# Infinite-attention then low-rank mixer on one core: scores of a pair in one row-tiled stretch, PSUM as one ring of eight banks, down tiles whole

## The chip, the core and the metric

One of the cores of a Trainium2 chip runs the whole program. The metric is the device time of one execution in microseconds (us), as the median of several runs. A profile is one more execution, with the trace taken by the hardware profiler; it has a time of its own, and the span in it is from the first to the last instruction.

The engines are named as in the profile: PE is TensorE (PEld its weight loads), DVE is VectorE, ACT is ScalarE, POOL is GpSimd, SP is SyncE, which issues most of the DMAs. Each engine works through its instructions in program order; what it waits for comes from the others over semaphores.

## The reference

Attention over 4 batches and 8 heads, with 768 positions and 64 channels a head, where a position sees only the first 8 positions and the 96 last ones, with a linear bias; its output, with the heads side by side (768 x 512 a batch), goes through a mixer: a low-rank product along the sequence (rank 32) is added, then an MLP of 512 to 2048 to 512 with ReLU is added.

```python
scores = scale * np.matmul(q, k.transpose(0, 1, 3, 2))
keep = is_global | is_local          # first 8 keys, or the 96 last ones
scores = np.where(keep, scores + bias, -1000000000.0)
a = softmax(scores)                  # over the keys
x = heads_side_by_side(a @ v)        # (4, 768, 512)
...
h = x.transpose(0, 2, 1) @ U @ V
u = x + h.transpose(0, 2, 1)
out = u + np.maximum(u @ w_ch1, 0.0) @ w_ch2
```

## The kernel before

**Pairs.** Two heads of one batch, which fill 128 partitions as 2 x 64, are a pair: 16 pairs, numbered i, four (NP) a batch. The sequence is six blocks of 128. A block of queries needs the scores of its own block and, for the blocks 1 to 5, those of a block kA that holds the block before it, with the global keys copied over its first rows. That is 11 tiles of 128 x 128 for each head, kept side by side as 1408 columns, computed in three chunks (512, 512, 384 columns).

**One pair's steps.** `st_T` (for the pairs up to 7) turns q and k with matmuls and copies them out of PSUM; `turn` and `st_K` do that for the later ones with DMA transposes. `scores` (L320) writes a chunk of both heads to two PSUM banks. The matmuls of the heads contract over 64 rows, one over the upper, one over the lower half of the array, and are issued in turn. Pairs 0 to 3 add the bias on PE and take the exponential straight from PSUM (`st_SE`); for the pairs 4 to 15, `s_dve` (L366) adds it on DVE while it writes the chunk to SBUF, and `st_E` (L378) takes the exponential of a whole head on ACT. `st_V` (L383) multiplies by v, with a column of ones for the sum: 11 matmuls of 65 columns a head, then a reciprocal (L399), a multiply (L407) on DVE and a cast to f16 on POOL (L408).

**The mixer's steps.** `st_M1` (L411) multiplies a pair's 128 channels by U, six matmuls, and DVE copies the result out. `st_M3` (L450) multiplies that by V, six matmuls into two banks, adds it on DVE to x (L462), and POOL casts the sum (L465). U and V hold rank 32 in 128 rows, the rest zeros. `st_X` (L443) turns the cast sum with a DMA transpose into uT. The MLP of half a batch (g) is 16 up tiles and 3 down tiles. An up tile (L480) is four matmuls of 384 columns, with a ReLU on ACT (L484). A down tile (L500) is 16 matmuls of 512 columns, cut into four parts, or for the last tile into two halves of the columns; DVE adds x (L506) and SP sends the block out. Batch 0 has one matmul more in every down tile, for its V product.

**The order.** It is written out by hand, and `manual_schedule` keeps it. The prologue (L569 to L610) does the attention of batch 0; it also computes chunk 0 of pair 4. The loop over i from L614 does the steps of pair i, `st_V` and `st_M1` and `st_M3` and `st_X` of pair i - 1, and between them calls `fill(n)`, which issues n pieces from two queues: up tiles, and parts of down tiles. `queue_ff` fills the queues; a batch's pieces are queued when all of its pairs have been turned into uT, for batch b in the iteration of pair 4b + 5. `held` keeps the down tiles back until the iteration of pair 7. Up tiles may run ahead of the down tiles of the half before (`room`), and `ahead` deals about four ups to three parts. What is left after the loop is issued in its order.

**PSUM.** Eight banks in four groups: `sc` 2, `ob` 1 (the output of `st_V`), `cps` 2 (down tiles), `th` 3 (everything else: transposes, up tiles, U and V products). A tile waits until the bank of its group that was taken longest ago has been read.

Of the kernel before, what the change touches and what calls it, by code (L numbers as in the profile page):

```python
# [20 lines left out]
def kernel(  # L21
# [13 lines left out]
    nc = tc.nc  # L35
# [38 lines left out]
    def ps_sc(tag="sc"):  # L74
        return psum.tile([P, 512], FP32, name="sc", tag=tag, bufs=2)

    def ps_ob():
        return psum.tile([P, 512], FP32, name="ob", tag="ob", bufs=1)

    def ps_cps(name):  # L80
        return psum.tile([P, 512], FP32, name=name, tag="cps", bufs=2)

    def ps_th(name, dtype=FP32, cols=512):
        return psum.tile([P, cols], dtype, name=name, tag="th", bufs=3)

# [64 lines left out]
    def warm(n):  # L150
        wps = ps_cps("warm")
        for _ in range(n):
            nc.tensor.matmul(wps, zw[:, 0:P], zw, start=True, stop=True)
# [77 lines left out]
    def st_T(i):  # L231
# [4 lines left out]
        for st in (stq, stk):  # L236

            tp = ps_th("tp", FP16, S)
# [81 lines left out]
    def scores(i, c, on_pe):  # L320
        kT, kA, qT = kts[i], kas[i], qts[i]
        scs = [ps_sc("cps" if on_pe and (i + c) % 2 else "sc") for _ in range(2)]
        c0 = 512 * c
        tot = min(512, W - c0)
        r0 = 256 if c else 0
        if on_pe:
            for hi in range(2):
                nc.tensor.matmul(
                    scs[hi][:, 0:tot], slI[:, 2 * (i % NP) + hi],
                    rel16.rearrange("p a c -> p (a c)")[:, r0:r0 + tot], start=True, stop=False,  # L330
                )
        for kb in (2 * c, 2 * c + 1):
            o = 256 * kb - c0
            for hi in range(2):
                r = slice(hi * D, (hi + 1) * D)
                nc.tensor.matmul(  # L336
                    scs[hi][:, o:o + P], kT[r, kb * P:(kb + 1) * P], qT[r, kb * P:(kb + 1) * P],
                    start=(o == 0 and not on_pe), stop=(o + P == tot),
                )
            if kb == NSB - 1:  # L340
                continue
            for hi in range(2):
                r = slice(hi * D, (hi + 1) * D)
                nc.tensor.matmul(  # L344
                    scs[hi][:, o + P:o + 2 * P], kA[r, kb], qT[r, (kb + 1) * P:(kb + 2) * P],
                    start=False, stop=(o + 2 * P == tot),
                )
        return [(sc, c0, tot, r0) for sc in scs]

    def st_SE(i, c):  # L350
# [4 lines left out]
        for hi, (sc, c0, tot, _) in enumerate(scores(i, c, True)):  # L355
# [6 lines left out]
    def s_dve(i, hi, got):  # L362
        sc, c0, tot, r0 = got
        if c0 == 0:
            sps[i, hi] = scp.tile([P, W], FP32, name=f"sp{hi}", tag=f"sp{hi}", bufs=1)
        nc.vector.scalar_tensor_tensor(  # L366
            out=sps[i, hi][:, c0:c0 + tot], in0=sc[:, 0:tot],
            scalar=qk_scale / slope[2 * (i % NP) + hi], in1=relf[:, r0:r0 + tot],
            op0=ALU.mult, op1=ALU.add,
        )  # L370

    def st_S(i, c):
        for hi, got in enumerate(scores(i, c, False)):
            s_dve(i, hi, got)
# [8 lines left out]
    def st_V(i, hi):  # L383
        b, h = i // NP, 2 * (i % NP) + hi
        ep, vt, vA = eps.pop((i, hi)), vts[i], vas[i]
        obf = ps_cps("ob") if (i, hi) == (NP - 1, 1) else ps_ob()
# [24 lines left out]
    def st_M1(i):  # L411
        b, dc = i // NP, i % NP
        ch = slice(dc * P, (dc + 1) * P)
        tps = ps_th("tmp_ps")
        for n in range(NSB):
            nc.tensor.matmul(  # L416
                tps[:, 0:P], u16[:, n], x16s[b][:, dc, n],
# [4 lines left out]
    def st_M2(i):  # L422
        b, dc = i // NP, i % NP
        ch = slice(dc * P, (dc + 1) * P)
        for g in range(2):
            ups = ps_th("ups")
# [23 lines left out]
    def st_M3(i):  # L450
        b, dc = i // NP, i % NP
        ch = slice(dc * P, (dc + 1) * P)
        for g in range(2):
            ups = ps_th("ups")
            for t in range(NTG):
                n = NTG * g + t
                nc.tensor.matmul(  # L457
                    ups[:, t * P:(t + 1) * P], v16w[:, n * P:(n + 1) * P], tmps[b][:, ch],
                    start=(t == 0), stop=(t == NTG - 1),
                )  # L460
            dst = xs[b][:, NTG * g:NTG * (g + 1), ch]
            nc.vector.tensor_tensor(  # L462
                dst, ups[:, 0:GT].rearrange("p (t d) -> p t d", t=NTG), dst, ALU.add
            )
        nc.gpsimd.tensor_copy(x16s[b][:, dc], xs[b][:, :, ch])  # L465
# [3 lines left out]
    def queue_ff(b, g):  # L469
# [4 lines left out]
        def mk_up(jt):  # L474
            def go():
                if jt == 0:
                    cell["htr"] = ffp.tile([P, NJC, GT], FP16, name="htr", tag="htr")
                hps = ps_th("hps")
# [8 lines left out]
        def mk_down(t, part):  # L487
            n = NTG * g + t

            def go():  # L490
                if part == 0:
                    cell["cps"] = ps_cps("cps")
                    if b == 0:
                        nc.tensor.matmul(
                            cell["cps"], v16w[:, n * P:(n + 1) * P], tmp16,
                            start=True, stop=False,
                        )
                cps, htr = cell["cps"], cell["htr"]
                for jc in range(4 * part, 4 * part + 4):
# [4 lines left out]
                if part == NJC // 4 - 1:  # L504
                    osb = ffp.tile([P, DM], FP32, name="osb", tag="osb", bufs=3)
                    nc.vector.tensor_tensor(osb, cps, x_sb[:, n], ALU.add)  # L506
                    nc.sync.dma_start(out[b, n * P:(n + 1) * P, :], osb)
            return go

        def mk_last(t, half):  # L510
            n = NTG * g + t
            cs = slice(half * (DM // 2), (half + 1) * (DM // 2))

            def go():
                cps = ps_cps("cps")[:, 0:DM // 2]
                htr = cell["htr"]
                for jc in range(NJC):
                    nc.tensor.matmul(  # L518
                        cps, htr[:, jc, t * P:(t + 1) * P], w2_16[:, jc, cs],
                        start=(jc == 0), stop=(jc == NJC - 1),  # L520
                    )
                osb = ffp.tile([P, DM], FP32, name="osb", tag="osb", bufs=3)
                nc.vector.tensor_tensor(osb[:, cs], cps, x_sb[:, n, cs], ALU.add)
                nc.sync.dma_start(out[b, n * P:(n + 1) * P, cs], osb[:, cs])
# [4 lines left out]
        for t in range(NTG):  # L529
            if (b, g, t) == (B - 1, 1, NTG - 1):  # L530
                for half in range(2):
                    downs_q.append((mk_last(t, half), (b, g)))
                continue
            for part in range(NJC // 4):
                downs_q.append((mk_down(t, part), (b, g)))

    ahead, held = [0], [True]

    def fill(n):
        for _ in range(n):  # L540
            down = downs_q and not held[0] and not any(w == downs_q[0][1] for _, w in ups_q)
            room = ups_q and (not downs_q or downs_q[0][1] == ups_q[0][1]
                              or ups_q[0][1] in follows(downs_q[0][1]))
            if down and room:
                if ahead[0] > 0:
                    ahead[0] -= 4
                    downs_q.popleft()[0]()
                else:
                    ahead[0] += 3
                    ups_q.popleft()[0]()  # L550
            elif down:
                downs_q.popleft()[0]()
            elif room:
                ups_q.popleft()[0]()
            else:
# [48 lines left out]
    first = scores(NP, 0, False)  # L604
# [4 lines left out]
    for hi in range(2):  # L609
        s_dve(NP, hi, first[hi])  # L610
# [3 lines left out]
    for i in range(NP, NPAIR + 2):  # L614
        b, hp = divmod(i, NP)
        live = i < NPAIR
        n = 1 if i < 2 * NP + 1 else 2
# [11 lines left out]
        if i == NP + 1:  # L629
            load_qk(NP + 4)  # L630
        fill(2)
# [17 lines left out]
        if i > NP + 1 and (i - 2) % NP == NP - 1:  # L649
            queue_ff((i - 2) // NP, 0)  # L650
            queue_ff((i - 2) // NP, 1)
            ahead[0] = 1
        if i == NPAIR + 1:
            break
        fill(n)
        if live:
            st_S(i, 2)
            if i < NPE:
                st_P(i)
        if i + 1 < NPAIR:  # L660
            if i + 1 >= NPE:
                st_K(i + 1)
# [5 lines left out]
        fill(1)  # L668
        if i > NP:
            st_M1(i - 1)  # L670
        if live:
            st_E(i, 0)
        fill(2)
        if i > NP:
            st_M3(i - 1)
            st_X(i - 1)
        if live:
            st_E(i, 1)
        if i + 2 < NPAIR and i + 2 >= NPE:
            turn(i + 2)  # L680
        fill(1 + n)
# [38 lines left out]
```

## Time and profile before

| | us |
|---|---|
| runs, median of 3 | 245.56 (245.24 to 245.64) |
| the profiled execution | 243.5 |
| its span | 241.6 |
| PE busy | 228.9 |
| DVE busy | 126.7 |
| ACT busy | 114.2 |
| POOL busy | 79.0 |

The page divides the span into 40 slices of 6.04 us, and gives the busy share of each engine in tenths. PE is at 8 or 9 in nearly all of them; DVE, ACT and POOL are busiest in the first half, while there are pairs to do, and nearly idle at the end, where only the MLP is left. A busy PE counts the time from a matmul's start to its modelled end, so that matmuls that follow one another overlap; the distance from one start to the next tells more. In a group's line, the columns are line, engine, operation, output and inputs, shape and count, then busy us and mean ns of one, then the idle time of the engine before them and what ended most of it. In a timeline's line they are start, length, the group, and, in brackets, idle time before it and what ended that.

### The profile page before, as it was taken

The numbers are of one execution on the slowest core, as the hardware profiler recorded it, in microseconds if no ns is written. First come the engines' busy times: TensorE is split into PE (matmuls) and PEld (weight loads), VectorE is DVE, ScalarE is ACT, GpSimd is POOL, SyncE is SP. The second block draws the span as 40 slices with busy tenths as digits, with TensorE's granted clock in tenths as the row PEclk, the third lists the DMA queues.
The fourth block names the chain that finished last, engine by engine and source line by source line (L and its number), as shares of the span: only waits on it lengthen the run. The fifth ranks groups of instructions, "written<-read, shape, count | busy, mean of one in ns | idle before, by whom it ended". The sixth has DMA issues, their size and how long they took to land.

```text
span 241.6 us, 4863 instructions
## 1 busy us (share of the span) xinstructions
PE 228.9 (95%) x1952; PEld 127.9 (53%) x1952; DVE 126.7 (52%) x269; ACT 114.2 (47%) x196; POOL 79.0 (33%) x122
## 2 busy tenths in 40 slices
PE   7789899889999999999999999999999999999994
PEld 3355654555554545555555555555565555555553
DVE  6878975848486867565747574745432111011121
ACT  6686548676650403765453407482733234543300
POOL 6379837657272524151515142212111000000000
PEclk9999999999999999999999999999999999999999
DMA  6999999999596979985949582721121200111022
GB/s 186 314 309 324 226 241 272 197 230 217 116 207 148 236 216 161 240 198 136 241 111 212 150 230 69 184 56 37 57 67 33 87 34 12 43 43 42 7 85 87
DMA packets 86030, 36.61 MB, mean 152 GB/s; under 512 B 74136, under 2 KB 82552, under 8 KB 86008
## 3 DMA queue, kind: packets, MB, share of 16 engines
q1 hardware_dynamic: 81480, 32.01, 53.2%
q0 software_dynamic: 4528, 4.29, 10.9%
q8 instruction: 15, 0.25, 0.4%
q14 instruction: 7, 0.06, 0.1%
HBM read 27.46 MB, written 6.29 MB: 140 GB/s over the span
## 4 chain that ended last, share of the span: by engine, by line
PE 76%; DMA 9%; POOL 5%; ACT 5%; DVE 2%; issue 2%; SPq 0%; POOLq 0%
PE cps L500 33%; PE hps L480 31%; DMA w<-in_moe_w_ch_dram 5%; PE sc L336 3%; DMA vst<-in_v_dram 3%; ACT ep L378 2%; ACT htr L484 2%; PE ob L394 2%; DMA kst<-in_k_dram 2%; PE cps L518 1%; PE ob L390 1%; PE tmp_ps L416 1%; POOL v L126 1%; POOL vA L277 1%; PE sc L344 1%
## 5 line engine op out<-in xcount | busy, mean ns | idle before, releaser
L484 ACT ACTIVATE htr<-hps 128x384 f16<-128x384 f32 x128 | 61.8, 491 | 88.6 <-PE hps L480 87.4
L480 PE MATMUL hps<-uT,w 128*128 128x384 f16 x512 | 98.2, 326 | 1.2 <-ACT htr L484 0.8
L500 PE MATMUL cps<-w,htr 128*128 128x512 f16 x368 | 90.8, 379 | 0.0
L480 PEld LDWEIGHTS <-w 128*128 128x128 f16 x512 | 46.7, 98 | 34.9 <-issue 2.1
L366 DVE SCALAR_TENSOR_TENSOR sp<-sc,relcat 128x512 f32<-128x512 f32 (+1 forms) x72 | 43.2, 642 | 28.7 <-PE sc L344 23.8
L500 PEld LDWEIGHTS <-htr 128*128 128x128 f16 x368 | 34.2, 98 | 33.6
L506 DVE TENSOR_TENSOR osb<-cps,x_sb 128x512 f32<-128x512 f32 x23 | 15.9, 691 | 50.7 <-PE cps L500 50.5
L378 ACT ACTIVATE ep<-sp 128x1408 f16<-128x1408 f32 x24 | 32.7, 1372 | 12.6 <-DVE sp L366 12.6
L408 POOL CAST x<-x_sb 128x384 f16<-128x384 f32 x30 | 15.4, 513 | 60.0 <-DVE x_sb L407 59.8
L465 POOL CAST x<-x_sb 128x768 f16<-128x768 f32 x12 | 9.9, 829 | 34.1 <-DVE x_sb L462 34.1
L462 DVE TENSOR_TENSOR x_sb<-ups,x_sb 128x384 f32<-128x384 f32 x24 | 12.5, 554 | 11.0 <-PE ups L457 10.6
L336 PEld LDWEIGHTS <-kT 64*128 64x128 f16 x192 | 8.2, 93 | 17.6 <-issue 15.6
L407 DVE TENSOR_TENSOR x_sb<-ob,rcp 128x384 f32<-128x384 f32 x30 | 16.7, 558 | 1.0
L336 PE MATMUL sc<-qT,kT 64*128 64x128 f16 x192 | 16.5, 221 | 0.0
L394 PE MATMUL ob<-v,ep 128*128 128x65 f16 x192 | 16.0, 193 | 0.0
L394 PEld LDWEIGHTS <-ep 128*128 128x128 f16 x192 | 13.8, 98 | 2.7 <-issue 0.2
L126 POOL CAST v<-vst 128x768 f16<-128x768 f32 x16 | 13.4, 839 | 5.5 <-DMA vst<-in_v_dram 5.5
L356 ACT ACTIVATE ep<-sc 128x512 f16<-128x512 f32 (+1 forms) x24 | 12.0, 560 | 4.8 <-PE sc L344 3.5
L344 PE MATMUL sc<-qT,kA 64*128 64x128 f16 x160 | 14.2, 216 | 0.0
L390 PE MATMUL ob<-vA,ep 128*128 128x65 f16 x160 | 14.1, 194 | 0.1
L112 POOL CAST k<-kst 128x768 f16<-128x768 f32 x14 | 12.1, 867 | 0.1
L390 PEld LDWEIGHTS <-ep 128*128 128x128 f16 x160 | 11.0, 97 | 2.1
(73 smaller groups left out, 166.3 us busy)
## 6 DMA issues: line engine op xcount, KB each, us to landing
qst<-in_q_dram SPq DMA_DIRECT2D x16, 384.0 KB, 4.0
kst<-in_k_dram SPq DMA_DIRECT2D x16, 384.0 KB, 5.7
vst<-in_v_dram SPq DMA_DIRECT2D x16, 384.0 KB, 5.9
out_dram<-osb SPq DMA_DIRECT2D x23, 256.0 KB, 2.3
w<-in_moe_w_ch_dram POOLq DMA_DIRECT2D x6, 512.0 KB, 8.7
vA<-v SPq DMA_DIRECT2D x8, 152.3 KB, 3.9
w<-in_moe_w_ch_dram POOLq DMA_DIRECT2D x1, 1024.0 KB, 11.6
out_dram<-osb SPq DMA_DIRECT2D x2, 128.0 KB, 1.7
```

The lines of the kernel that those rows point to most:

```text
L126: nc.gpsimd.tensor_copy(vt.rearrange("p n h d -> p h n d")[:, :, :, 0:D], vsts.pop(i).rearrange("p (h n) d -> p h n d", h=2),)
L336: nc.tensor.matmul(scs[hi][:, o:o + P], kT[r, kb * P:(kb + 1) * P], qT[r, kb * P:(kb + 1) * P], start=(o == 0 and not on_pe), stop=(o + P ...
L344: nc.tensor.matmul(scs[hi][:, o + P:o + 2 * P], kA[r, kb], qT[r, (kb + 1) * P:(kb + 2) * P], start=False, stop=(o + 2 * P == tot),)
L366: nc.vector.scalar_tensor_tensor(out=sps[i, hi][:, c0:c0 + tot], in0=sc[:, 0:tot], scalar=qk_scale / slope[2 * (i % NP) + hi], in1=relf[:, ...
L378: nc.scalar.activation(ep, sps.pop((i, hi)), AF.Exp, scale=slope[2 * (i % NP) + hi])
L390: nc.tensor.matmul(ob[:, qi], ep[:, OF[qi - 1]:OF[qi - 1] + P], vA[:, qi - 1, hi], start=True, stop=False,)
L394: nc.tensor.matmul(ob[:, qi], ep[:, DG[qi]:DG[qi] + P], vt[:, qi, hi], start=(qi == 0), stop=True,)
L407: nc.vector.tensor_tensor(xo, ob[:, :, 0:D], rb, ALU.mult)
L480: nc.tensor.matmul(hps[:, 0:GT], w1_16[:, dc, jt * P:(jt + 1) * P], uT[:, dc, ts], start=(dc == 0), stop=(dc == NDC - 1),)
L484: nc.scalar.activation(cell["htr"][:, jt], hps[:, 0:GT], AF.Relu)
L500: nc.tensor.matmul(cps, htr[:, jc, t * P:(t + 1) * P], w2_16[:, jc], start=(b > 0 and jc == 0), stop=(jc == NJC - 1),)
L506: nc.vector.tensor_tensor(osb, cps, x_sb[:, n], ALU.add)
```

## The change

PSUM becomes one ring of eight banks: every tile, whatever it is for, takes the bank that was taken longest ago, through `bank`. A new function `visit(i, m)` does the V product of pair m = i - 2 and then all 22 score matmuls of pair i, without another matmul between them; the V product reads copies of U and V (`ud`, `vd`) in which rank 32 stands twice, from row 0 and from row 64, so that its two banks are written by matmuls over 64 rows each, issued in turn. It takes up to eight banks: two for the V product and six for the scores. DVE reads them in the order: the two of the V product, the three of head 0, the three of head 1. The cast and the DMA transpose of the V product's sum (`st_C`, `st_X`) are issued in iteration m + 2, behind `st_V` of pair i - 1. Down tiles are issued whole. `fill` becomes `ff(units)`: an up tile counts one unit, a down tile five; a down tile is taken when five ups have been issued since (`since`), when there is no up to take, or when the call asks for one first. An iteration calls `ff` with n, n, n, 1 and n units, where n is 2 up to pair 9 and 3 from there. A batch's pieces are queued at the end of the iteration of pair 4b + 5. Chunk 0 of pair 4 leaves the prologue. The diff, cut to its core:

```diff
+    def bank(name, dtype=FP32, cols=512):
+        return psum.tile([P, cols], dtype, name=name, tag="ps", bufs=8)
...
+    ud = cst.tile([P, NSB, P], FP16, name="ud")
+    vd = cst.tile([P, S], FP16, name="vd")
...
+    def operands(i, hi, t):
+        r = slice(hi * D, (hi + 1) * D)
+        kb, off = t // 2, t % 2
+        key = kas[i][r, kb] if off else kts[i][r, kb * P:(kb + 1) * P]
+        return key, qts[i][r, (kb + off) * P:(kb + off + 1) * P]
...
+    def visit(i, m):
+        NB = 2 * NSB - 1
+        if m is not None:
+            bm, dm = m // NP, m % NP
+            ch = slice(dm * P, (dm + 1) * P)
+            ups = [bank("ups") for _ in range(2)]
+            for t in range(NTG):
+                for g in range(2):
+                    r, n = slice(g * D, (g + 1) * D), NTG * g + t
+                    nc.tensor.matmul(
+                        ups[g][:, t * P:(t + 1) * P], vd[r, n * P:(n + 1) * P], tmps[bm][r, ch],
+                        start=(t == 0), stop=(t == NTG - 1),
+                    )
+            for g in range(2):
+                dst = xs[bm][:, NTG * g:NTG * (g + 1), ch]
+                nc.vector.tensor_tensor(
+                    dst, ups[g][:, 0:GT].rearrange("p (t d) -> p t d", t=NTG), dst, ALU.add
+                )
+        if i is None:
+            return
+        got = []
+        for c in range(3):
+            got.append([bank("sc") for _ in range(2)])
+            for t in range(4 * c, min(4 * c + 4, NB)):
+                for hi in range(2):
+                    o = (t % 4) * P
+                    nc.tensor.matmul(
+                        got[c][hi][:, o:o + P], *operands(i, hi, t),
+                        start=(o == 0), stop=(t % 4 == 3 or t == NB - 1),
+                    )
+        for hi in range(2):
+            sp = scp.tile([P, W], FP32, name=f"sp{hi}", tag=f"sp{hi}", bufs=1)
+            sps[i, hi] = sp
+            for c in range(3):
...
+                nc.vector.scalar_tensor_tensor(
...
+    def st_C(i):
+        b, dc = i // NP, i % NP
+        nc.gpsimd.tensor_copy(x16s[b][:, dc], xs[b][:, :, dc * P:(dc + 1) * P])
...
         for t in range(NTG):
...
+            last = (b, g, t) == (B - 1, 1, NTG - 1)
+            downs_q.append(((mk_last if last else mk_down)(t), (b, g)))
+
+    since, held = [0], [True]
+
+    def can_down():
+        return downs_q and not held[0] and not any(w == downs_q[0][1] for _, w in ups_q)
+
+    def can_up():
+        return ups_q and (not downs_q or downs_q[0][1] == ups_q[0][1]
+                          or ups_q[0][1] in follows(downs_q[0][1]))
+
+    def ff(units, down_first=False):
+        while units > 0:
+            if can_down() and (down_first or since[0] >= 5 or not can_up()):
                 downs_q.popleft()[0]()
+                since[0], down_first = max(0, since[0] - 5), False
+                units -= 5
+            elif can_up():
+                ups_q.popleft()[0]()
+                since[0] += 1
+                units -= 1
             else:
                 return
...
     for i in range(NP, NPAIR + 2):
         b, hp = divmod(i, NP)
         live = i < NPAIR
-        n = 1 if i < 2 * NP + 1 else 2
+        m = i - 2 if i - 2 >= NP else None
+        n = 2 if i < 2 * NP + 2 else 3
         held[0] = i < NP + 3
...
-        if live and i > NP:
-            st_S(i, 0)
-        early = {NP: (NP + 2,), NP + 1: (NP + 3,), NP + 2: (NP + 5,)}
+        if i == NP:
+            ff(2)
+        if i <= NPAIR:
+            visit(i if live else None, m)
+        else:
+            visit(None, m)
+        early = {NP: (NP + 2,), NP + 1: (NP + 3, NP + 4), NP + 2: (NP + 5,)}
         for j in early.get(i, (i + 3,)):
             if j < NPAIR:
                 load_qk(j)
         if i + 1 < NPAIR:
             load_v(i + 1)
-        if i == NP + 1:
-            load_qk(NP + 4)
-        fill(2)
+        ff(n, True)
         if NP < i <= NPAIR:
             st_V(i - 1, 0)
         if i + 1 < NPE:
             st_T(i + 1)
         if live:
             cast_v(i)
             st_A(i)
...
-        fill(n)
+        ff(n)
         if live:
-            st_S(i, 1)
-        fill(1)
+            st_E(i, 0)
         if NP < i <= NPAIR:
             st_V(i - 1, 1)
+        if live and i < NPE:
+            st_P(i)
+        if m is not None:
+            st_C(m)
+            st_X(m)
...
+        ff(n)
         if live:
+            st_E(i, 1)
+        if i + 1 < NPAIR and i + 1 >= NPE:
+            st_K(i + 1)
         if i + 2 < NPAIR:
             cast_qk(i + 2, nc.gpsimd)
         if i == NP:
             load_w2(0)
             load_w2(1)
+            nc.gpsimd.memset(vd.bitcast(I32), 0)
+            nc.gpsimd.memset(ud.rearrange("p n c -> p (n c)").bitcast(I32), 0)
+            for r in (0, D):
+                nc.gpsimd.dma_start(vd[r:r + R], moe_V)
+                nc.gpsimd.tensor_copy(ud[:, :, r:r + R], u16[:, :, 0:R])
-        fill(1)
+        ff(1)
-        if i > NP:
+        if NP < i <= NPAIR:
             st_M1(i - 1)
-        if live:
-            st_E(i, 0)
-        fill(2)
-        if i > NP:
-            st_M3(i - 1)
-            st_X(i - 1)
-        if live:
-            st_E(i, 1)
         if i + 2 < NPAIR and i + 2 >= NPE:
             turn(i + 2)
-        fill(1 + n)
+        if m is not None and m % NP == NP - 1:
+            queue_ff(m // NP, 0)
+            queue_ff(m // NP, 1)
+        ff(n)
```

More of the change, by code (lines that the diff above doesn't have):

```diff
@@ L150, in warm @@
     def warm(n):
-        wps = ps_cps("warm")
+        wps = bank("warm")
         for _ in range(n):
@@ L318, with scores @@
     sps, eps, later = {}, {}, []
-    def scores(i, c, on_pe):
+    def scores(i, c):
         kT, kA, qT = kts[i], kas[i], qts[i]
-        scs = [ps_sc("cps" if on_pe and (i + c) % 2 else "sc") for _ in range(2)]
+        scs = [bank("sc") for _ in range(2)]
         c0 = 512 * c
@@ L425, in st_M2 @@
         for g in range(2):
-            ups = ps_th("ups")
+            ups = bank("ups")
             nc.tensor.matmul(
@@ L477, in go @@
                     cell["htr"] = ffp.tile([P, NJC, GT], FP16, name="htr", tag="htr")
-                hps = ps_th("hps")
+                hps = bank("hps")
                 for dc in range(NDC):
@@ L485, in mk_up, with mk_down @@
             return go
-        def mk_down(t, part):
+        def mk_down(t):
             n = NTG * g + t
             def go():
[L491 to L499, printed above, removed]
+                cps, htr = bank("cps"), cell["htr"]
+                if b == 0:
+                    nc.tensor.matmul(
+                        cps, v16w[:, n * P:(n + 1) * P], tmp16, start=True, stop=False,
+                    )
+                for jc in range(NJC):
                     nc.tensor.matmul(
@@ L503, in go, with mk_last @@
                     )
[L504 to L507, printed above, removed]
+                osb = ffp.tile([P, DM], FP32, name="osb", tag="osb", bufs=3)
+                nc.vector.tensor_tensor(osb, cps, x_sb[:, n], ALU.add)
+                nc.sync.dma_start(out[b, n * P:(n + 1) * P, :], osb)
             return go
[L510 removed]
+        def mk_last(t):
             n = NTG * g + t
[L512 removed]
             def go():
[L515 removed]
                 htr = cell["htr"]
[L517 to L521, printed above, removed]
[L522 to L524 removed]
+                osb = ffp.tile([P, DM], FP32, name="osb", tag="osb", bufs=3)
+                for half in range(2):
+                    cs = slice(half * (DM // 2), (half + 1) * (DM // 2))
+                    cps = bank("cps")[:, 0:DM // 2]
+                    for jc in range(NJC):
+                        nc.tensor.matmul(
+                            cps, htr[:, jc, t * P:(t + 1) * P], w2_16[:, jc, cs],
+                            start=(jc == 0), stop=(jc == NJC - 1),
+                        )
+                    nc.vector.tensor_tensor(osb[:, cs], cps, x_sb[:, n, cs], ALU.add)
+                    nc.sync.dma_start(out[b, n * P:(n + 1) * P, cs], osb[:, cs])
             return go
```

121 lines of the change are left out of this document (23 added, 98 removed).

## The prediction

> **What bounds the kernel now.** I read the page first (busy shares, the 40 slices, the chain), then TensorE's timeline, then the other engines in one iteration. The page's lines are engine shares, chain shares, and two groups with count, busy us, mean ns:
>
> ```profile
> span 241.6 us, 4863 instructions
> PE 228.9 (95%) x1952; PEld 127.9 (53%) x1952; DVE 126.7 (52%) x269; ACT 114.2 (47%) x196; POOL 79.0 (33%) x122
> ...
> PE 76%; DMA 9%; POOL 5%; ACT 5%; DVE 2%; issue 2%; SPq 0%; POOLq 0%
> ...
> L480 PE MATMUL hps<-uT,w 128*128 128x384 f16 x512 | 98.2, 326 | 1.2 <-ACT htr L484 0.8
> L500 PE MATMUL cps<-w,htr 128*128 128x512 f16 x368 | 90.8, 379 | 0.0
> ```
>
> TensorE is the bound; the mean ns of one matmul overlap their neighbours, so I price by start-to-start. The timeline around pair 12's first score chunk (start, length, group):
>
> ```profile
> 123.12 1.03 PE L500 MATMUL cps<-w,htr 128*128 128x512 f16 x4
> 124.08 0.23 PE L336 MATMUL sc<-qT,kT 64*128 64x128 f16 x2
> 124.14 0.22 PE L344 MATMUL sc<-qT,kA 64*128 64x128 f16 x2
> 124.20 0.22 PE L336 MATMUL sc<-qT,kT 64*128 64x128 f16 x2
> 124.26 0.22 PE L344 MATMUL sc<-qT,kA 64*128 64x128 f16 x2
> 124.41 0.82 PE L480 MATMUL hps<-uT,w 128*128 128x384 f16 x4
> ```
>
> Two 64-row matmuls run beside each other, a pair of them every 0.056 us. Four down matmuls take 4 x 0.216, so the first would be through at 123.98; the next full-height matmul starts at 124.41. The chunk costs 0.43: 4 x 0.056 = 0.22 of work and 0.20 for going in and out of row tiling. Likewise a chunk of six is 0.37, an up tile (four matmuls) 0.65, a down tile 16 x 0.216 = 3.46, a V step (11 matmuls of 65 columns) 0.34, U product and V product (six matmuls each) 0.34, an st_T 0.68.
>
> From 32.08 (first up) to 238.1 (last matmul issued) are 206.0 us. Adding these prices over all work of that stretch gives 200.0, so about 6.0 are idle, more than half before 62 us; the rest are three waits of 0.8 of the second V product for a bank that an htr holds.
>
> **The saving.** Before, a pair pays 0.43 + 0.43 + 0.37 + 0.34 = 1.57 for scores and V product. After: one stretch of 0.20 + (11 + 3) x 0.056 = 0.98. That is 0.59 for ten pairs (6 to 15), 0.41 for pair 5 (no V product yet), nothing for pair 4 (a chunk lay in the prologue, where the U product waits for DVE anyway), and -0.03 for each of the last two V products, which switch by themselves. Sum 6.2. The new work is 193.9: 128 ups 83.2, 24 downs 84.2, 24 V steps 8.2, 12 U products 4.1, three st_T 2.0, stretches 12.2.
>
> **The fill, where it fails.** In program order, the new `ff` gives (u = up, D = whole down tile): pairs 4 to 6, 11, 9, 9 u. Pair 7: D, D, D, u, uu. `since` stands at 29 by then, so every call takes a D, which counts 5 against a budget of 1 to 3 and overshoots. Pair 8: D, D, D, then nothing: batch 0 is used up. Pair 9: nothing until batch 1 is queued at its end, then uu. Before, the parts were dealt one by one and the last of batch 0 came in pair 9 itself. Pair 13 likewise: D, D, nothing, then uuu. Pair 17 has D, D, which cover its chain.
>
> So in pair 9 the new end of the chain lies open, since the V product of pair 7 moved there from pair 8, and with it the cast and transpose that the ups need. The rows for it, in the old pair 9 (DVE, POOL, SyncE; then microseconds to landing):
>
> ```profile
> 91.18 1.29 DVE L366 SCALAR_TENSOR_TENSOR sp<-sc,relcat 128x512 f32<-128x512 f32 x2 [1.22 <-PE sc L344]
> 92.49 0.20 DVE L399 RECIPROCAL rcp<-ob 128x6 f32<-128x6 f32 x1
> 92.72 0.56 DVE L407 TENSOR_TENSOR x_sb<-ob,rcp 128x384 f32<-128x384 f32 x1
> ```
> ```profile
> 90.48 0.84 POOL L126 CAST v<-vst 128x768 f16<-128x768 f32 x1
> 93.34 0.51 POOL L408 CAST x<-x_sb 128x384 f16<-128x384 f32 x1 [2.02 <-DVE x_sb L407]
> 98.28 0.83 POOL L465 CAST x<-x_sb 128x768 f16<-128x768 f32 x1 [2.88 <-DVE x_sb L462]
> ```
> ```profile
> uT<-x SPq DMA_TRANSPOSE x12, 2.8
> ```
>
> DVE is in order, and the stretch hands it eight evictions before both halves of pair 8: two adds at 0.47, four score tiles at 0.60, two at 0.46 = 4.3; then reciprocal and multiply, 0.78 a half: 5.1 and 5.9. POOL: first half 5.6, cast of v 6.4, second half 6.9 (the U product of pair 8 waits for it), cast of pair 7 at 7.7. SyncE first issues the two vA transfers (0.94 + 0.79) behind the cast of v, so the transpose starts at 8.2 and lands at 11.0. Only then can an up start.
>
> **Walk.** Pairs 4 to 6: idle of 5.4 by the same kind of sum: banks wait for the second head's evictions (0.5 and 1.1, at st_T), a stretch waits for ACT behind an exponential (0.8), the U products wait for POOL (1.35 and 1.6). Pair 7 starts at 63.3, where it started at 63.21 with one up more behind it. The new POOL work of pair 4 (two memsets of 0.42, two DMA issues of 0.68, two small copies between 0.2 and 0.7) lies ahead of pair 4's casts, which wait for DVE until about its end; it costs up to 0.6, inside the 1.35. Moving load_qk(8) ahead of load_v(6) on SyncE costs nothing while vst(6) has an iteration in hand. Pair 7 is 0.98 + 3 x 3.67 + 0.68 + 1.95 + 0.34 = 15.0, pair 8 13.0: 91.3. Pair 9's V product needs the U product just issued: DVE finishes an osb and the copy first, 0.9. Its adds start at 92.5, so the ups start at 103.5 (before: 93.16). From the stretch's end at 93.2, TensorE has 1.0 of work and 9.3 idle.
>
> Pair 13, from the stretch's end: D, V step, D, V step end at 7.6; the second osb ends at 8.15, second half 8.95, POOL 9.45 and 10.3, landing 13.1: idle 5.2 net of a U product. Pairs 10, 12, 14 have only ups: the stretch holds all eight banks, and after three ups the V step needs the bank of head 1's first tile, the fourth score eviction in DVE's order, free at 2.7 against 1.95: 0.75 each. At their ends, ACT lags behind its second exponential and the next stretch, which needs every bank back, waits 0.5, 0.2 and 0.5. Sum 3.45, with everything behind TensorE in its queue held. Other little waits 0.3.
>
> **Clock.** Before never leaves TensorE idle for over 1.3 us, so a gap of 9 is not in its trace. The one row after nothing at all is the start (start, length):
>
> ```profile
> 1.20 3.59 PE L153 MATMUL warm<-zw 128*128 128x512 f16 x8 [1.20 <-DVE zw L148]
> ...
> 6.13 0.59 PE L153 MATMUL warm<-zw 128*128 128x512 f16 x2
> ```
>
> Eight took 3.59, about twice 8 x 0.216; soon after they were at full rate. A restart costs 0 to 1.8; I take 1.8 for pair 9's gap, the one most like the start, and none for pair 13's.
>
> The Trainium skill, TensorE: Matmul & The Clock Gate, Part 1, says that the clock is halved after an idle window of about 3.4 us and restored after a busy one. By that rule, the estimate is the same for pair 9, and pair 13, with quiet stretches of 1.9 and 3.3 us, may or may not pay too; the trace of before agrees at its start, with the 3.59 above, and shows no other case.
>
> **Sum.** Idle after: 5.4 + 0.9 + 9.3 + 5.2 + 3.45 + 0.3 + 1.8 = 26.4. End of the matmuls: 32.1 + 193.9 + 26.4 = 252.4, 14.2 later than 238.1; the tail is unchanged. The profiled execution took 243.5 (span 241.6), so it becomes 257.7; the runs' median was 245.56, 2.1 above it, so I forecast 245.56 + 14.2 = **259.8**.
>
> **Rivals.**
> - Faster: TensorE stays fed, idle stays near 6.0, and the saving shows: 245.56 - 6.2 = 239.4. The shares of DVE (52%) and POOL (33%) speak for it. It decides at an idle of 6.0 + 6.2 = 12.2: the chain of pair 9 alone would have to fall from 11 to about 5 and pair 13's to vanish. The order of the queues speaks against. Chance 0.06.
> - The clock also falls in pair 13's gap: 261.6. For it: its U product is only 0.34 of work in 5.5. Chance 0.18.
> - The ring waits in every iteration, not in three: the stretch needs all eight banks back, and an exponential with three htr behind it is 1.37 + 3 x 0.43 = 2.7. At about 1 more in eight visits: 268. Against: a D ends ACT's backlog in pairs 7, 8, 11, 12, 15. Chance 0.11.
> - The stretch doesn't do what it says: matmuls into two banks, or V product tiles of 32 filled rows in 64, pair no better than full height, and the 6.2 is lost: 266. The 0.056 rows above speak against. Chance 0.04.
> - Gaps as forecast, but without clock and half of the ring and early waits: about 253.5; part of the forecast's low side.
>
> **Numbers.** Forecast 0.61 (254 to 265). Its unknowns: landing, counted from the issue's end, 1.2 later at both gaps (+2.4); clock -1.8 to +1.8; pairs 4 to 6 and ring, half to double (-4.4 to +4.4 and more). The range 253.5 to 266.0 leaves out the fast rival and the ring in every iteration. Faster by over 0.2% (what a measurement here can tell from none) 0.06, within 0.02, slower 0.92.
>
> **What would show it.** Right: TensorE quiet for 8 to 11 us between pair 9's stretch and batch 1's first up, released by the uT transpose; again 4 to 6 us in pair 13; stretches of 0.98; V steps after three ups that wait for DVE sc. Wrong: ups or downs in pair 9's gap; transposes landing within 6 us of the stretch; stretches much over 1 us with no wait on a bank.

## The result and the profile after

The changed kernel takes 268.49 us in the median (265.8 to 270.44), the one before 245.4: a ratio of 1.0917, with a 95% interval of 1.0812 to 1.1022. It is slower, as forecast, but by 23 us where 14 were forecast, and outside the range. The profiled execution took 267.54. Each ratio, here and below, is to the kernel before, run again beside the changed one. The ratios leave out executions that took over 1.5% more than the fastest of the same kernel, the medians do not.

The page of the changed kernel, in the same places as before (busy shares; the granted clock in 40 slices of 6.64 us; the chain; the two large groups):

```profile
span 265.8 us, 4860 instructions
PE 231.9 (87%) x1952; PEld 132.8 (50%) x1952; DVE 123.6 (46%) x269; ACT 113.8 (43%) x196; POOL 80.1 (30%) x128
...
PEclk9999999958999997599999998599999997999999
...
PE 58%; DMA 17%; POOL 9%; issue 7%; DVE 6%; SPq 2%; POOLq 0%; DVEq 0%
...
L484 PE MATMUL hps<-uT,w 128*128 128x384 f16 x512 | 96.6, 342 | 9.3 <-DMA uT<-x 8.6
L501 PE MATMUL cps<-w,htr 128*128 128x512 f16 x368 | 82.5, 379 | 0.2
```

The number of matmuls is the same, but PE's share of the chain fell from 76% to 58%, and DMAs, POOL and "issue" took it. The up tiles now wait 8.6 us for uT. New is the clock: it drops in four places, and a busy PE is then a slow one. So PE's time has to be split before it says anything. I take the distance from each matmul's start to the next and subtract the prices at full clock that the prediction used; what is left over is lost, and the trace tells to what. From the first up tile on, in us:

| | before | after |
|---|---|---|
| matmuls at full clock | 192.6 | 190.8 |
| in and out of row tiling | 7.6 | 2.7 |
| half clock | 0 | 7.7 |
| waits and the rest | 5.7 | 28.5 |

The change does what it says: 1.8 of matmul time and 4.9 of switching are gone, 6.7 together. The waits and the clock take 30.5 more. (A wait counted by this split is up to 0.4 longer than the idle time in a line's brackets, which counts from the modelled end of the matmul before.)

**Pairs 5 and 6.** TensorE from 51 us on (in brackets the idle time before the group and what ended it), then POOL's queue ahead of it, and the time from issue to landing of vd:

```profile
51.12 0.49 PE L433 MATMUL tmp_ps<-x,ud 128*128 128x128 f16 x6 [2.45 <-POOL x L424]
51.45 2.16 PE L484 MATMUL hps<-uT,w 128*128 128x384 f16 x8
56.29 0.84 PE L358 MATMUL ups<-tmp,vd 64*128 64x128 f16 x6 [2.68 <-DMA vd<-in_moe_V_dram]
```
```profile
42.82 1.57 POOL L209 DMA_DIRECT2D w<-in_moe_w_ch_dram  x2
...
45.12 0.53 POOL L664 DMA_DIRECT2D vd<-in_moe_V_dram  x1
...
46.02 0.49 POOL L664 DMA_DIRECT2D vd<-in_moe_V_dram  x1
```
```profile
vd<-in_moe_V_dram POOLq DMA_DIRECT2D x2, 48.0 KB, 10.8
```

The V product of pair 4 waits for 48 KB. They were issued behind two parts of w2 on POOL's queue and took 10.8 us to land.

**Pair 9.** TensorE from the stretch's last scores to batch 1's first ups:

```profile
98.67 0.24 PE L375 MATMUL sc<-qT,kT 64*128 64x128 f16 x2
105.36 0.80 PE L433 MATMUL tmp_ps<-x,ud 128*128 128x128 f16 x6 [5.41 <-POOL x L424]
105.95 1.17 PE L484 MATMUL hps<-uT,w 128*128 128x384 f16 x3
109.63 1.76 PE L484 MATMUL hps<-uT,w 128*128 128x384 f16 x5 [2.52 <-DMA uT<-x]
```

This is the forecast gap. Between 98.67 and 105.36 only two V steps run (their lines are left out); the U product waits for POOL; then three matmuls of an up tile run, on the three quarters of uT that are there, and the fourth waits for the transpose. It landed 11.7 after the stretch began at 97.94.

**Pair 13.** Two down tiles and two V steps end by about 161.0; then come the same two waits, shorter:

```profile
162.72 0.49 PE L433 MATMUL tmp_ps<-x,ud 128*128 128x128 f16 x6 [1.74 <-POOL x L424]
163.05 0.65 PE L484 MATMUL hps<-uT,w 128*128 128x384 f16 x3
166.27 1.12 PE L484 MATMUL hps<-uT,w 128*128 128x384 f16 x3 [2.57 <-DMA uT<-x]
```

**Pair 17.** SyncE, then TensorE:

```profile
209.31 7.62 SPq L507 DMA_DIRECT2D out_dram<-osb  x3
217.02 1.25 SPq L462 DMA_TRANSPOSE uT<-x  x1
```
```profile
208.76 7.08 PE L501 MATMUL cps<-w,htr 128*128 128x512 f16 x32
215.67 0.65 PE L484 MATMUL hps<-uT,w 128*128 128x384 f16 x3
219.82 4.50 PE L484 MATMUL hps<-uT,w 128*128 128x384 f16 x18 [3.49 <-DMA uT<-x]
```

POOL's cast had ended at 211.2. But the transpose stands in SyncE's queue behind the output of the two down tiles, and the second of these is ready only at 216.6. The fill that was to hide the chain held it up.

**The clock.** Stretches of the span: length, then busy us and counts of PE, PEld, DVE, ACT and POOL, then the granted clock, DMA share and GB/s:

```profile
51.00:56.30 5.30, 2.50 (x15) 1.19 (x14) 0.29 (x1) 0.98 (x2) 2.34 (x4) 0.60 1.20 200
56.30:63.00 6.70, 6.64 (x63) 4.72 (x64) 5.40 (x11) 1.66 (x3) 0.51 (x1) 0.55 1.21 216
63.00:98.00 35.00, 33.20 (x272) 17.96 (x271) 19.13 (x42) 12.62 (x17) 14.20 (x21) 1.00 0.78 168
...
105.40:113.00 7.60, 5.08 (x43) 3.05 (x43) 1.36 (x4) 0.98 (x2) 2.21 (x3) 0.50 0.80 185
...
166.00:172.00 6.00, 5.73 (x43) 3.16 (x43) 2.15 (x5) 1.47 (x3) 0.00 (x0) 0.54 0.59 134
```

After each quiet place the clock is granted at half. The spells in the trace run from 52.1 to 62.3, 103.3 to 113.5, 164.7 to 171.5 and 219.3 to 222.7: about 10.2, 10.2, 6.8 and 3.4 us.

### The profile page after: what moved, and what is told of

Same layout as the page of the kernel before. It is cut to its first block, busy times and chain, and to the rows that moved or that the text cites. A ratio compares the mean times of both kernels' runs of the same rounds, so it can differ in the third digit from the quotient of the medians.

```text
span 265.8 us, 4860 instructions
## 1 busy us (share of the span) xinstructions
PE 231.9 (87%) x1952; PEld 132.8 (50%) x1952; DVE 123.6 (46%) x269; ACT 113.8 (43%) x196; POOL 80.1 (30%) x128
## 4 chain that ended last, share of the span: by engine, by line
PE 58%; DMA 17%; POOL 9%; issue 7%; DVE 6%; SPq 2%; POOLq 0%; DVEq 0%
PE cps L501 26%; PE hps L484 24%; DMA w<-in_moe_w_ch_dram 4%; DMA vst<-in_v_dram 4%; DMA vd<-in_moe_V_dram 4%; DMA uT<-x 3%; DVE sp L386 3%; DMA kst<-in_k_dram 2%; POOL v L116 2%; PE sc L375 1%; PE ups L358 1%; PE cps L520 1%; POOL q L102 1%; DVE x_sb L364 1%; PE ob L410 1%
## 5 line engine op out<-in xcount | busy, mean ns | idle before, releaser
L484 PE MATMUL hps<-uT,w 128*128 128x384 f16 x512 | 96.6, 342 | 9.3 <-DMA uT<-x 8.6
L488 ACT ACTIVATE htr<-hps 128x384 f16<-128x384 f32 x128 | 60.6, 493 | 98.1 <-PE hps L484 97.6
L501 PE MATMUL cps<-w,htr 128*128 128x512 f16 x368 | 82.5, 379 | 0.2
L484 PEld LDWEIGHTS <-w 128*128 128x128 f16 x512 | 50.2, 101 | 44.0 <-issue 15.6
L501 PEld LDWEIGHTS <-htr 128*128 128x128 f16 x368 | 35.5, 97 | 41.0
L506 DVE TENSOR_TENSOR osb<-cps,x_sb 128x512 f32<-128x512 f32 x23 | 15.9, 692 | 76.7 <-PE cps L501 76.4
L386 DVE SCALAR_TENSOR_TENSOR sp<-sc,relcat 128x512 f32<-128x512 f32 (+1 forms) x72 | 40.8, 636 | 1.3 <-PE sc L375 1.3
L433 PE MATMUL tmp_ps<-x,ud 128*128 128x128 f16 x72 | 6.3, 226 | 10.1 <-POOL x L424 10.1
L116 POOL CAST v<-vst 128x768 f16<-128x768 f32 x16 | 13.4, 837 | 5.6 <-DMA vst<-in_v_dram 5.6
L375 PE MATMUL sc<-qT,kT 64*128 64x128 f16 x144 | 11.8, 239 | 0.4 <-ACT htr L488 0.4
L102 POOL CAST q<-qst 128x768 f16<-128x768 f32 x14 | 11.6, 827 | 0.1
```

Of the source, the lines that this page charges most:

```text
L102: eng.tensor_copy(st16.rearrange("p n h d -> p h n d"), st)
L116: nc.gpsimd.tensor_copy(vt.rearrange("p n h d -> p h n d")[:, :, :, 0:D], vsts.pop(i).rearrange("p (h n) d -> p h n d", h=2),)
L386: nc.vector.scalar_tensor_tensor(out=sp[:, c0:c0 + tot], in0=got[c][hi][:, 0:tot], scalar=qk_scale / slope[2 * (i % NP) + hi], in1=relf[:, ...
L484: nc.tensor.matmul(hps[:, 0:GT], w1_16[:, dc, jt * P:(jt + 1) * P], uT[:, dc, ts], start=(dc == 0), stop=(dc == NDC - 1),)
L488: nc.scalar.activation(cell["htr"][:, jt], hps[:, 0:GT], AF.Relu)
L501: nc.tensor.matmul(cps, htr[:, jc, t * P:(t + 1) * P], w2_16[:, jc], start=(b > 0 and jc == 0), stop=(jc == NJC - 1),)
```

## The experiments

The theory after the result: the fill runs out (pairs 9 and 13), the chain to uT stands late in the queues (pairs 9, 13, 17), vd stands behind w2 (pair 4's V product), and each quiet place is paid a second time through the clock. The rivals: the gaps cost their length alone; attention's chain would hold TensorE anyway; or the ring, which every stretch asks for whole, is the cost.

### vd ahead of w2

```diff
         if i == NP:
-            load_w2(0)
-            load_w2(1)
             nc.gpsimd.memset(vd.bitcast(I32), 0)
...
+            load_w2(0)
+            load_w2(1)
```

> After the change 268.5. Edit: the two small loads of V into vd (with their memsets and copies) are issued ahead of the two w2 loads on the same queue instead of behind them; nothing else. Theory (the small loads queue behind 1 MB of weights): the 3.05 us wait of pair 4's V product goes, and with it the spell at half clock from 52 to 62, which costs 2.7; pair 4's U product still waits 2.6 for POOL. So about 5 less, 263.5 (261 to 265.5). Rival (the V product would wait there anyway, for the U product or for banks): within 1 of 268.5.

264.63 us, ratio 1.0811 (1.0757 to 1.0866). The time is within what was expected, but its interval meets that of the change (1.0812 to 1.1022), so that the trace is what settles the cause. vd lands in 4.5 us instead of 10.8,

```profile
vd<-in_moe_V_dram POOLq DMA_DIRECT2D x2, 48.0 KB, 4.5
```

and nothing waits for it. Part of the gain goes again: the U product of pair 5 now waits 1.6 for POOL, where it waited 0.5. What was not expected: the spell of half clock does not go, it shrinks to 52.9 to 56.3. The 2.5 us in which pair 4's U product waits for POOL are enough for one.

### Zeros in the quiet places

```diff
         ff(1)
+        if i in (9, 13):
+            warm(24 if i == 9 else 8)
         if NP < i <= NPAIR:
             st_M1(i - 1)
+        if i in (9, 13, 17):
+            warm({9: 12, 13: 12, 17: 16}[i])
```

> After the change 268.5. Edit: matmuls of zeros, read by nobody, fill the quiet stretches of TensorE in the iterations of pairs 9, 13 and 17 (5.2 + 2.6, 1.7 + 2.6 and 3.5 us at full clock); what waits for what stays. Theory (a quiet stretch costs a second time, through the clock): gaps keep their length, no half clock there; the trace after the change puts that cost at 0.7 + 1.1 (pair 9), 1.8 (13), 1.4 (17), so 5.0 less: 263.5 (261.5 to 265). Rival (the gaps cost their length alone): 268.5 or up to 1 more.

261.87 us, ratio 1.0722 (1.0662 to 1.0782): 6.6 less in the medians, and an interval clear of the change's. TensorE has more to do, in the places of the zeros nothing comes earlier, and the kernel is faster: the clock's price is shown. From pair 9's first scores to the last matmul, the profile went from 164.1 to 159.0, the 5 that were expected. What the medians show beyond that is not the zeros' doing as far as the profile tells: ahead of the first of them, the V product of pair 4 waits 1.5 for vd in this execution, instead of 2.7. In pair 9's place the profile has the zeros, then the same wait for the same transpose:

```profile
99.17 5.34 PE L143 MATMUL warm<-zw 128*128 128x512 f16 x24
104.48 0.49 PE L433 MATMUL tmp_ps<-x,ud 128*128 128x128 f16 x6
104.81 2.75 PE L143 MATMUL warm<-zw 128*128 128x512 f16 x12
107.40 0.65 PE L484 MATMUL hps<-uT,w 128*128 128x384 f16 x3
108.99 0.97 PE L484 MATMUL hps<-uT,w 128*128 128x384 f16 x5 [0.94 <-DMA uT<-x]
```

### Cast and transpose right behind the stretch

```diff
             visit(None, m)
+        if m is not None:
+            st_C(m)
+            st_X(m)
...
         if live and i < NPE:
             st_P(i)
-        if m is not None:
-            st_C(m)
-            st_X(m)
```

> After the change 268.5. Edit: the cast and the transpose of the V product's sum are issued right behind the stretch, ahead of the iteration's down tiles, V steps and loads; the dealing of the fill stays. Theory (the place of the chain in POOL's and SyncE's queues sets the size of the gaps): the waits of the ups for uT (2.9, 2.7 and 3.65) go, those of the U products (5.6 and 1.9) stay, and about half of the clock's cost there (4.5) goes: about 11 less, 257.5 (255 to 260.5). Rival (only the missing fill counts): the ups still start when the U product is through, and nothing else is gained in pair 17: 265 to 268.

252.59 us, ratio 1.0344 (1.0301 to 1.0387): 16 less, more than the 11 expected. No up waits for uT any more, in all three places; the U products still wait 5.6 (pair 9) and 1.9 (pair 13), as expected. The miss has two parts. From pair 9's first scores to the last matmul, the profile is 13.4 shorter (150.7), because the clock, which I had counted at half, gained more: the spells for pairs 13 and 17 went whole. Another 2.3 lies ahead of pair 9, most of it before the moved chain first runs: there the wait for vd was 1.8 in this execution, and the half clock behind it shorter, which is luck. In all the clock's cost fell from 7.7 to 3.2. In pair 9 POOL now does the cast first, and the last thing to be late is the half that the U product needs:

```profile
97.90 0.83 POOL L469 CAST x<-x_sb 128x768 f16<-128x768 f32 x1 [3.47 <-DVE x_sb L364]
101.84 0.51 POOL L424 CAST x<-x_sb 128x384 f16<-128x384 f32 x1 [3.12 <-DVE x_sb L423]
102.30 0.84 POOL L116 CAST v<-vst 128x768 f16<-128x768 f32 x1
```

### The overshoot carried on

```diff
-        while units > 0:
+        credit[0] += units
+        while credit[0] > 0:
...
-                units -= 5
+                credit[0] -= 5
...
-        n = 2 if i < 2 * NP + 2 else 3
+        n = 2 if i < 2 * NP else 3
```

> After the change 268.5. Edit: what a down tile takes over the budget of a call is carried into the next calls, and n is 3 from pair 8; the order of everything else stays. Batch 0 then lasts to the end of pair 9, batch 1 to pair 14. Theory (the fill runs out in pairs 9 and 13): the waits of 5.6 and 1.9 (U products) go, those for uT (2.9 and 2.7) shrink to 0 to 2 each, pair 17 has ups to do (3.65 goes), and of the clock's cost 5.0 goes: about 251.5 (248.5 to 255). Rival (attention's chain through DVE, POOL and ACT sets the iteration's length, so that TensorE waits elsewhere): 262 or more.

253.32 us, ratio 1.0359 (1.031 to 1.0408). Within the expectation: with the order of everything else kept, batch 0 lasts, and the waits of 5.6 and 1.9 are gone. New ones came, of V products for DVE (2.1, 0.7 and 0.7) and of the U product of pair 5 for POOL (2.3). One wait for uT stays in pair 9, a little longer than expected, because there the transpose is issued only at 101.9, behind the loads, an output and the two vA transfers on SyncE's queue:

```profile
100.67 0.65 PE L484 MATMUL hps<-uT,w 128*128 128x384 f16 x3
104.69 1.49 PE L484 MATMUL hps<-uT,w 128*128 128x384 f16 x5 [3.37 <-DMA uT<-x]
```

### The three together

> The three edits of the first, third and fourth experiment together: vd loaded ahead of w2, cast and transpose right behind the stretch, overshoot of a down tile carried on. Before 244.9, after 268.5, the even deal alone 253.3. Theory (waits of TensorE and its clock explain the time, and the three causes add up): from the even deal go the last wait for uT (3.5), that for vd (0.7) and about 2 of the clock's cost: 247 (245 to 249.5), still not under the kernel before, because the U products of pairs 4 and 5 wait 2.6 and 2.5 for POOL and the V products behind an empty call wait for DVE (2.2, 0.8, 0.8). Rival (the ring of eight banks, asked for whole by each stretch, is a cost of its own): 251 or more.

248.64 us, ratio 1.0135 (1.0069 to 1.0201), within the expectation. Counted wait by wait from the even deal, the causes add up, and neither uT nor vd is waited for. The gains of the three experiments by themselves (3.9, 15.9 and 15.2) do not: the chain's place and the deal take away some of the same waits, and together the three bring 19.9. Left are above all the U products of pairs 4 and 5 (2.5 each) and V products behind an empty call (1.8, 0.8, 0.8).

### Dealt by hand

The fill of each iteration is a list of its five calls (u = up, D = down), and in pairs 5 to 7 POOL does the cast of v and vA later.

```diff
+    deal = {
+        4: "uu uu uu u uu", 5: "uu uu uu u u", 6: "uu uu uu u u",
+        7: "D - D - u", 8: "D u u u uD", 9: "D - D - uu",
+        10: "uuu uuu uuu u uuu", 11: "uD u u u uu", 12: "D u u u uu", 13: "D uu uu u u",
+        14: "D uu uu u uu", 15: "D uu uu u uu", 16: "D uu D u u", 17: "D uu uu u u",
+    }
...
-        if live:
+        if live and (i == NP or i >= NPE):
             cast_v(i)
             st_A(i)
...
             st_V(i - 1, 1)
+        if NP < i < NPE:
+            cast_v(i)
+            st_A(i)
```

> As the three together, but the fill is written out by hand, so that every U product is followed by an up or a down tile and nearly every iteration mixes both, and in pairs 5 to 7 POOL does the cast of v and the copy vA behind the cast that the U product waits for. Theory: the waits for POOL and DVE named above go too; what the row-tiled stretch saves (the traces after and before: 4.9 of switching, 1.8 of matmul time) then shows: 240.5 (238.5 to 243), under the kernel before at 244.9. Rival (the ring, or attention's chain through DVE and POOL, takes the place of the waits): 245 or more.

244.4 us, ratio 0.9998 (0.9967 to 1.0029): level with the kernel before, and short of the expectation. The rival holds in part. The later vA made DVE's small copy into it late, and that stands ahead of the U product's copy, for which the next V product waits (DVE, pair 5):

```profile
52.02 0.29 DVE L282 COPY vA<-v 8x520 f16<-8x520 f16 x1 [2.47 <-POOL vA L269]
52.23 0.27 DVE L437 CAST tmp<-tmp_ps 128x128 f16<-128x128 f32 x1
53.01 1.02 DVE L364 TENSOR_TENSOR x_sb<-ups,x_sb 128x384 f32<-128x384 f32 x2 [0.51 <-PE ups L358]
```

### The V product at full height

```diff
-                        ups[g][:, t * P:(t + 1) * P], vd[r, n * P:(n + 1) * P], tmps[bm][r, ch],
+                        ups[g][:, t * P:(t + 1) * P], v16w[:, n * P:(n + 1) * P], tmps[bm][:, ch],
```

> As dealt by hand, but the V product of the stretch runs at full height from the old U and V (no ud, no vd, none of their loads, memsets and copies); the scores stay in one stretch. Theory (six V product matmuls take 0.34 at full height and 0.17 in row tiling): ten stretches get 0.17 longer, the last two V products, which no longer switch, 0.03 shorter each: 1.3 to 1.7 more than dealt by hand, less what POOL gains in pair 4, so +0.5 to +1.7. Rival (the gain lies in the scores' single stretch alone): within 0.3 of it or faster.

Ratio 1.0067 (1.0029 to 1.0105) against 0.9998 of dealt by hand: 0.0069 of 245 is 1.7 us, the upper end of what was expected. The medians (247.49 and 244.4) lie further apart, and the intervals meet, so that the sign is likely and the size is not settled. Nor is the cause. By the split, matmuls and switching take 1.6 more in its profile, as was worked out, but the waits 1.5 less. Its one execution with the clock granted in full took 244.03, against 243.64 to 244.26 in three such of dealt by hand; the other eleven were granted 0.979 to 0.993. The difference in time may come from spells of half clock and not from the V product's height.

### More of the fill behind the U products

```diff
-        4: "uu uu uu u uu", 5: "uu uu uu u u", 6: "uu uu uu u u",
+        4: "uu uu uu u u", 5: "uu uu uu u u", 6: "uu uu u u u",
-        7: "D - D - u", 8: "D u u u uD", 9: "D - D - uu",
-        10: "uuu uuu uuu u uuu", 11: "uD u u u uu", 12: "D u u u uu", 13: "D uu uu u u",
+        7: "D - D - uuu", 8: "D u u uu D", 9: "D - D - uu",
+        10: "uuu uuu uuu u uuu", 11: "uD u u uu u", 12: "D u u uu uu", 13: "D uu uu u u",
...
-        if live and i < NPE:
-            st_P(i)
...
             st_M1(i - 1)
+        if live and i < NPE:
+            st_P(i)
```

> As dealt by hand (244.4), with more of the fill behind the U products of pairs 7, 11 and 12 or ahead of them, one up fewer in pairs 4 and 6, and in pairs 5 to 7 DVE's small copy into vA behind the copy of the U product, which it held up. Theory (what keeps that version from showing the saving are the waits of V products for DVE, 1.2, 1.7 and 1.45, and of U products for POOL, 3 x 0.9): 4 to 5 less, 240 (238.5 to 242.5). Rival (something else, such as the ring or the clock, takes it back): 243 or more.

241.52 us, ratio 0.9871 (0.9826 to 0.9916): within the expectation, and faster than both kernels. No V product waits any more.

### The stretch broken up

```diff
             got.append([bank("sc") for _ in range(2)])
+            if c:
+                nc.tensor.matmul(
+                    got[c][0][:, 0:64], zw[:, 0:P], zw[:, 0:64], start=True, stop=True,
+                )
```

> As the one before it, with one full-height matmul of zeros (64 columns, overwritten by the scores) between the first and second and between the second and third chunk of every stretch: the mode is switched two times more in each of 12 pairs, and nothing else is added. Theory (going in and out of row tiling costs 0.20 of TensorE's time): 24 x (0.20 + 0.03) = 5.5 more (4.5 to 6). Rival (the switch hides behind loads or other waits): under 2 more.

243.17 us, ratio 0.9912 (0.9875 to 0.995): 1.0 by the ratios and 1.7 by the medians over the one before, with intervals that meet, where 4.5 to 6 were expected. The rival holds, though the price of the switch was right. Around a break (pair 14), TensorE loses what was said: from 148.89 to 149.18 are 0.29, of which a pair of scores is 0.056.

```profile
148.89 0.22 PE L379 MATMUL sc<-qT,kA 64*128 64x128 f16 x2
149.04 0.20 PE L373 MATMUL sc<-zw 128*128 128x64 f16 x1
149.18 0.27 PE L379 MATMUL sc<-qT,kT 64*128 64x128 f16 x2
```

By the same split as above, switching rises from 3.2 to 7.9, and what is left of the waits falls from 9.1 to 3.9. From the first up to the last matmul, the two profiles take 203.1 and 203.4, nearly the same; the rest of their difference (1.5) lies ahead of the first up, where nothing was changed. In these two profiles, then, the switching that is saved comes back as waits. Some of these are for banks that DVE or ACT must read first. The unbroken version has three groups of them (what waits, for what; us in total, times, longest):

```profile
PE hps L484 <- DVE sp L386: 1.5, 1, 1.5
...
PE sc L375 <- ACT htr L488: 1.2, 6, 0.3
...
PE cps L497 <- DVE x_sb L364: 0.9, 1, 0.9
```

The scores' wait for ACT, which comes six times, is gone from the list of the broken one; the two others fall to 0.6 and 0.4. That is 2.6 of the 5.2, and it fits a stretch that, unbroken, is done before the banks that it and the next tiles need have been read. Another 1.0 was a V step's wait for vA, which has nothing to do with banks, and the remainder is not traced.

## Why the prediction was right and wrong

**Right in sign and cause.** The fill ran out in the pairs that were named. Pair 9's chain landed its transpose 11.7 after the stretch began; by the split above the gap lost 10.4 with its clock (forecast 9.3 + 1.8). Pair 13's waits lost 5.1 (forecast 5.2). The saving of 6.2 was 6.7. The fourth experiment, which changes the deal, and the third, which changes the chain's place, each take out what they should.

**Wrong in size.** The profiled execution was to be 257.7 and was 267.5. Three steps account for the difference:

| term | forecast | trace |
|---|---|---|
| pairs 4 to 6, waits, their clock included | 5.4 | 10.6 |
| pair 13, clock | 0 | 1.8 |
| pair 17, wait and clock | 0 | 3.7 + 1.4 |
| waits of ring and ACT, pairs 10 on | 3.75 | 2.0 |

- *"It costs up to 0.6, inside the 1.35"*: the new POOL work of pair 4 was priced by the time that POOL spends on issuing. The step missed that two of these issues are DMAs that stand behind the w2 loads, and that the V product waits for their landing: 3.05, and 2.7 of half clock in that place. The size is that of one execution: in the second, third and fourth experiments, which leave these loads as they are, the V product waits 1.5, 1.8 and 0.5 for vd. The prediction followed the other DMAs that were moved and not this one that was added.
- *"Pair 17 has D, D, which cover its chain"*: the chain was followed through POOL, but in SyncE's order it stands behind the outputs of those two tiles. The landing came 8.6 after POOL's cast, not 2.8.
- *Clock*: one restart was priced at 1.8, from the start of the program, and only for the longest gap. Four places paid, 7.7 in all. The rival with the clock in pair 13's gap too named this, at 261.6. The Trainium skill, TensorE: Matmul & The Clock Gate, Part 1, gives about 3.4 us as the length of an idle window that halves the clock and of the busy one that restores it. The spells here are one, two and three times that long, which agrees with the second. The waits that set them off were shorter than the first: 2.5 us in the first experiment, and 1.9 and 2.7 with a U product between them in pair 13.

**The ring** was neither harmless nor a cost in every iteration. In the changed kernel its waits were smaller than forecast (2.0). The V steps after three ups, which were to wait 0.75 each for the fourth score tile that DVE reads, do not wait: in pair 12 the V step starts at 141.5, while DVE reads the six tiles from 139.9 to 143.3, so it cannot need the bank that the forecast gave it. Once the large waits were gone, waits for banks were part of what held back the row-tiled stretch, as far as the last experiment shows; no run has the stretch without the ring, so the ring's own share is not measured. With all three causes mended and the fill dealt by hand, the gain over the kernel before is 1.3%, about 3 us, of the 6.7 that TensorE no longer spends.

## What to carry to other kernels

When filler work is counted out by budget, write down in program order where each batch of it ends; an item larger than its call's budget spends the filler of later calls, and a chain that was always hidden then lies open. Follow every DMA that a change adds or moves through its own queue to its landing, not only through the engine that issues it. And look for time saved on TensorE by a denser stretch among its waits: here about half of the saving came through, and part of the rest was waits for banks that had not been read yet.

## What was not expected of the hardware

- Half clock followed waits of TensorE that were shorter than its spells, but not each of them: 2.5 us was enough in the first experiment; in the three together the second of two such waits was followed by half clock, the first was not; in dealt by hand a spell begins at 15.4 us, after waits of only 0.6 and 0.7. The spells last 3.4, 6.8 or 10.2 us; in the first experiment, where TensorE was busy from 52.9 to 56.3, the one there was 3.4.
- In a kernel bound by TensorE, 72 matmuls of zeros in the quiet places of pairs 9, 13 and 17 made it 6.6 us faster in the medians, about 5 of it by the profile in these places.
- 48 KB landed 9.3 to 10.8 us after their issue behind two weight loads of 512 KB on the same queue (four profiles), and 3.6 to 4.5 us ahead of them (five).
